# Linear-recurrence scan and top-capacity expert layer on one core: the early slot's weight fetches, first gathers and tile places rearranged

## Chip, cores and metric

One core of a Trainium2 chip (trn2). The metric is the device time of one execution in microseconds; the profile beside it is of one execution of the same program.

## What is computed

```python
# x, f_logit: (4, 5056, 256); lower_bound: (256,); w_gate: (256, 8); w1: (8, 256, 1024); w2: (8, 1024, 256)
f = lower_bound + (1 - lower_bound) * sigmoid(f_logit)
for t in range(S):                      # per batch
    h = f[:, t] * h + (1 - f[:, t]) * x[:, t]
    y[:, t] = h
x = y.reshape(20224, 256)
logits = x @ w_gate
# all (token, expert) pairs by falling logit: a token takes the expert if both are free,
# each expert holds cap = 20224 // 8 = 2528 tokens
for e in range(8):
    out[assigned == e] = relu(x[assigned == e] @ w1[e]) @ w2[e]
```

## The kernel before

The work has two stages.

**Scan stage.** The 158 tiles of 128 tokens are cut into 40 chunks of four tiles (the last has two). For each chunk SP loads `f_logit` and `x` (512 KB each) into a pool `pin` of four buffers for each of the two. In iteration `i` the program writes `load(i + 3)`, `fwd(i)`, `sig(i + 2)` and `back(i - 1)`. `sig` is a sigmoid on ScalarE and then a product `xl <- fl, xl` on GpSimd. `fwd` transposes both on TensorE (`pf`, `pb`) and runs the recurrence as a scan on VectorE (`g <- fg, pb`). `back` transposes the result back with the gate's weights beside it (`pr`), and VectorE and ScalarE copy it into a row tile `hr` with 256 values and 8 logits per token; GpSimd copies the logits of a chunk into the table `X` (the logit copies, `X <- hr`). `store` writes an `hr` tile to the buffer `hbuf` in DRAM (528 KB, SP's queue). A ring of 22 places of 4,224 bytes a partition holds the `hr` tiles; half a store is written per chunk (`SR = 0.5`), so 17 chunks are stored when the loads end and 23 follow at the end.

**The early slot.** From the first 72 tiles (`CE`) the program picks the expert that has the fewest tokens above a limit and takes 896 rows of it ahead of the full routing. `prep` finds the best expert of a token in pieces (reduction, comparison, product with `kc` (on GpSimd), reduction, comparison); `prep_step(n)` does up to `n` of these pieces at the end of an iteration. When `prep` of 72 columns is through, the generator `early` runs one step per iteration: counts, index of the expert's weights, the three weight fetches (`first_weights`, indirect transfers from GpSimd, 2 MB in all), ranks, and row numbers in four groups. At the end four indirect gathers from `hbuf` bring the first 512 rows (`XGE`); they wait for the stores of chunks 0 to 17.

**Second stage.** Nine slots (the early one, -1, and the experts in order of their routing) are worked in chunks of four or so tiles. For each chunk: transposes (`pt`, split into `xh` and `xl`), eight steps of a first product (`pw`, evacuated by ScalarE into `hh` and by VectorE into `hl`) and a second (`py`), then `y` tiles (two tiles of rows in one) that indirect stores from GpSimd write to `out`. Weights are split into a high and a low part by ScalarE and VectorE (`w1h`, `w1l`, `w2s`). The order of TensorE, VectorE and ScalarE is written out by the program; a small planner (`Pace`) books each engine's time by a formula and decides from it where evacuations and the routing's steps (the search for each expert's limit on VectorE) are put. The order of this stage's GpSimd issues follows a list.

**Places.** The second stage's tiles lie where the ring and the scan's work tiles lay, so a tile waits until what lay there has been stored or read. Counted from the ring's start in places of 4,224 bytes, the program before has these chunks on them at the end of the scan stage:

```
place  0  1  2  3  4  5  6  7  8  9 10 11 12 13 14 15 16 17 18 19 20 21
chunk 22 26 29 31 33 35 37 39 19 21 20 18 38 36 34 32 30 28 27 25 24 23
```

The second stage's pools follow each other from the ring's start in the order in which they are opened: `wa2` (one `w2s` of 16,384 bytes, the early slot's) on places 0 to 3, then 13 `y` tiles of 2,080 bytes, then `wb` (32,768 bytes), `hp` (5 `hh` and 5 `hl` of 2,048) and `xp` (two `xh`, two `xl` of 4,096), the last of these on the scan's work tiles.

Of the kernel before, what the change touches and what calls it, by code (L numbers as in the profile page):

```python
# [7 lines left out]
F32 = mybir.dt.float32  # L8
F32R = mybir.dt.float32r
# [97 lines left out]
def kernel(ctx: ExitStack, tc: tile.TileContext, x: bass.AP, f_logit: bass.AP,  # L107
# [3 lines left out]
    nc = Paced(tc.nc, pace)  # L111
    B, S, D = x.shape
# [4 lines left out]
    P = 128  # L117
    NT = N // P
    NC = 160
    NG = NC // E  # L120
    KT = 4
    ROW = D + E
    FB = F // P
# [19 lines left out]
    NCH = len(chunks)  # L143
    RING = 22
    SR = 0.5
# [15 lines left out]
    def rows_tile(dt):  # L161
        return pin.tile([P, KT * ROW], dt, name="fl")
# [411 lines left out]
    def ranks(c0, c1):  # L574
        em = EM[:, c0:c1]
        v.tensor_scalar(em, A1[:, c0:c1], ecode, 0.0, op0=OP.is_equal, op1=OP.add, accum_out=ecnt)
        v.tensor_tensor_scan(RSE[:, RW - c1 + c0:RW], onec[:, c0:c1], em, 0.0, op0=OP.mult, op1=OP.add)
# [15 lines left out]
    def early(wi, ids):  # L593

        def sums(ps):
            for g in range(CE // 8):
                nc.tensor.matmul(ps[:, :64], ones_b, O[:, 8 * g:8 * g + 8].rearrange("p c e -> p (c e)"), start=(g == 0),
                                 stop=(g == CE // 8 - 1))
        yield sums
        ps = beside[0]  # L600
        v.tensor_reduce(SC8, ps[:, :64].rearrange("p (c e) -> p e c", e=E), AX.X, OP.add)
        v.tensor_scalar(Q8, SC8, float(EARLY), 1.0e6, op0=OP.is_lt, op1=OP.mult)
        v.tensor_tensor(Q8, Q8, SC8, op=OP.add)
        v.tensor_reduce(few, Q8, AX.X, OP.min)
        yield
        v.scalar_tensor_tensor(Q8, Q8, few, kc, op0=OP.is_equal, op1=OP.mult)
        v.tensor_reduce(ecode, Q8, AX.X, OP.max)
        v.scalar_tensor_tensor(wi, wk, ecode, wb, op0=OP.mult, op1=OP.add)
        first_weights()
        yield  # L610
        ranks(0, CE)
        yield
        w = CE + 2

        def places(ps):
            nc.tensor.matmul(ps[:, w:w + 1], tri, ecnt, start=True, stop=True)
            nc.tensor.matmul(ps[:, :w], nsub, RSE[:, RW + 2 - w:], start=False, stop=True, skip_group_check=True)
        yield places
        ps = beside[0]
        st = ohp.tile([P, len(groups)], F32, name="st")  # L620
        for k in range(2):
            v.tensor_scalar(st[:, k:k + 1], ps[:, w:w + 1], -512.0 * k, None, op0=OP.add)
        v.tensor_copy(RAE[:, :w], ps[:, :w])
        v.tensor_tensor(RAE[:, w - 2:w - 1], ecnt, ps[:, w - 3:w - 2], op=OP.subtract)
        v.tensor_scalar(elim, ps[:, w:w + 1], -1.0, float(EARLY), op0=OP.mult, op1=OP.add)
        yield
        g1 = {}
        nb = EARLY // P
        for b0 in range(0, nb, 2):
            n = min(2, nb - b0)  # L630
            if b0 % 4 == 0:
                g1 = ohp.tile([P, 512], BF, name="g1")
                v.tensor_scalar(g1, IO, st[:, b0 // 4:b0 // 4 + 1], None, op0=OP.is_ge)
                yield

            def rows(ps):
                for b in range(n):
                    nc.tensor.matmul(ps[:, b * w:(b + 1) * w], g1[:, (b0 + b) % 4 * P:((b0 + b) % 4 + 1) * P],
                                     RAE[:, :w], start=(b == 0), stop=(b == n - 1), skip_group_check=True)
            yield rows  # L640
            for _ in blocks(beside[0], b0, n, w, 0, ids[:, b0:b0 + n], False):
                pass
            if b0 + n < nb:
                yield
# [55 lines left out]
    def sig(i):  # L700
        np_ = chunks[i][2]
        for a, b in halves(0, i):
            nc.scalar.activation(FT[i][:np_, a:b], FT[i][:np_, a:b], AF.Sigmoid, scale=-1.0)
        for a, b in halves(1, i):
            (nc.gpsimd if i else nc.vector).tensor_mul(XT[i][:np_, a:b], FT[i][:np_, a:b], XT[i][:np_, a:b])
# [49 lines left out]
            nc.gpsimd.tensor_copy(X[:, t0:t0 + n], HR[i][:, :n, P:P + E])  # L755

    ST = {}

    def store(i):
        t0, n, _ = chunks[i]  # L760
        ST[i] = nc.sync.dma_start(hbuf[t0 * P:(t0 + n) * P].rearrange("(n p) d -> p n d", p=P), HR[i][:, :n])

    def prep(c0, c1):
        e = min(c1, NT)
        x_, t_, m_, a_ = X[:, c0:e], TMP[:, c0:e], M0[:, c0:e], A1[:, c0:e]
        far = nc.gpsimd if c1 <= 128 else v
        v.tensor_reduce(m_, x_, AX.X, OP.max)
        yield 'k'
        v.tensor_tensor(t_, x_, bcl(m_, e - c0), op=OP.is_ge)
        yield 'k'  # L770
        far.tensor_tensor(t_, t_, bce(kc, e - c0), op=OP.mult)
        yield 'k'
        v.tensor_reduce(a_, t_, AX.X, OP.max)
        yield 'k'
        v.tensor_tensor(O[:, c0:e], bce(kc, e - c0), bcl(a_, e - c0), op=OP.is_equal)
        yield 'k'

# [1 line left out]

    def prep_step(n):  # L780
        while preps and n:
            if next(preps[0], None) is None:
                preps.pop(0)
            else:
                n -= 1

    sig(0)
    nc.vector.tensor_scalar(omlb, lbc, -1.0, 1.0, op0=OP.mult, op1=OP.add)
# [11 lines left out]
    w1v = w1.rearrange("e d f -> (e d) f")  # L800
    w2v = w2.rearrange("e (p j) d -> (e p) (j d)", j=FB)

    def first_weights():
        for n, (dst, src) in enumerate(((RAWE[0][:, 0], w1v), (RAWE[0][:, 1], w1v),
                                        (RAWE[1].rearrange("p j d -> p (j d)"), w2v))):
            nc.gpsimd.indirect_dma_start(out=dst, out_offset=None, in_=src,
                                         in_offset=bass.IndirectOffsetOnAxis(ap=WIE[:, n:n + 1], axis=0))

    WSE = []

    XGE = None
    for i in range(NCH + 1):
        job = next(est, None) if est is not None else None
        if i + LA - 1 < NCH:
            load(i + LA - 1)
            if i == 0:
                nc.gpsimd.memset(rest[-1], 0.0)
        if i < NCH:
            fwd(i)
        if i + 2 < NCH:  # L820
            sig(i + 2)
        if i >= 1:
            back(i - 1, job)
            while stored < min(i - 1, int(SR * (i - 1))):
                store(stored)
                stored += 1
        if i >= 4:
            build(2)
        if i >= NCH - 2:
            if i < NCH:  # L830
                WSE.append(pin.tile([P, FB, P], F32R, name="xl"))
            for h, j0 in (((0, 0),), ((1, 0),), ((0, 4), (1, 4)))[i - NCH + 2]:
                nc.scalar.activation(WSE[h][:, j0:j0 + 4], RAWE[0][:, h].rearrange("p (q j) -> p j q", j=FB)[:, j0:j0 + 4],
                                     AF.Identity, scale=omlb[:, h:h + 1])
        if i == NCH - 2:
            assert stored * KT >= CE
            XGE = rows_tile(F32R)
            for q in range(KT):
                nc.gpsimd.indirect_dma_start(out=XGE[:, q * ROW:(q + 1) * ROW].bitcast(F32), out_offset=None,
                                             in_=hbuf[:CE * P],  # L840
                                             in_offset=bass.IndirectOffsetOnAxis(ap=IDE[:, q:q + 1], axis=0),
                                             bounds_check=NT * P - 1, oob_is_err=False)
        upto = chunks[i - 1][0] // 8 * 8 if i else 0
        if done < CE and (upto - done >= 32 or upto >= CE):
            preps.append(prep(done, min(upto, CE)))
            done = min(upto, CE)
        elif CE <= done < CP and upto >= done + 32:
            preps.append(prep(done, done + 32))
            done += 32
        prep_step(99 if i == NCH else 3 if done == CE and upto < CE + 8 else PS if done < CE else 1 + (i > NCH - 3))  # L850
        if est is None and done >= CE and not preps:
            est = early(WIE, IDE)
# [21 lines left out]
    def route(r, rt, slot, free):  # L874
# [40 lines left out]
        else:  # L915
# [18 lines left out]
            v.scalar_tensor_tensor(MS, asg, cc, TR, op0=OP.is_equal, op1=OP.mult, accum_out=cM)  # L934
            spawn()
            yield 'DVE',
    for i in range(stored, NCH):
        store(i)
    pre.close()
    sched.close()  # L940
# [8 lines left out]
def moe(ctx, tc, g):  # L949
# [9 lines left out]

    def pool(name, bufs, **kw):  # L960
        return ctx.enter_context(tc.tile_pool(name=name, bufs=bufs, reuse_waits="tile", **kw))
    wa2 = pool("wa2", 1)
    YB = 13
    yp = pool("yp", YB)
    wb_ = pool("wb", 1)
    hp = pool("hp", 5)
    xp = pool("xp", 2)

    def y_tile():
        return yp.tile([P, 2 * D + 8], F32, name="y")[:, :2 * D].rearrange("p (r d) -> p r d", r=2)  # L970

    def x_tile():
        return rows_tile(F32R).rearrange("p (q r) -> p q r", q=4)
# [50 lines left out]
    def split(k):  # L1024
# [3 lines left out]
        for t, name in ((w1h, "w1h"), (w1l, "w1l")):  # L1028
            for h in range(len(t), 2):
                t.append(pin.tile([P, FB, P], F32R, name="xl") if k % 2 else  # L1030
                         wb_.tile([P, FB, P], F32R, name=f"{name}{h}"))
        w2s = (wa2 if k % 2 else wb_).tile([P, FB, 2, D], F32R, name="w2s")
        WS[k] = w1h, w1l, w2s
        pieces = []
        for j0, h in ((0, 0), (0, 1), (4, 0), (4, 1)):
# [382 lines left out]
```

## Time and profile before

| | us |
|---|---|
| median of 3 runs | 1196.99 (1195.78 to 1198.12) |
| the profiled execution | 1195.04 |
| its span | 1193.3 |
| TensorE busy | 1153.3 (97%) |
| VectorE busy | 791.0 (66%) |
| ScalarE busy | 540.8 (45%) |
| GpSimd busy | 459.2 (38%) |

How to read it: PE is TensorE's matmuls, PEld its weight loads, DVE VectorE, ACT ScalarE, POOL GpSimd, SP the queue that issues loads and stores. Busy shares are means over both stages, and a busy TensorE is not one at its peak. Nearly all instructions carry one line number (L100, a helper), so the names of the tiles tell them apart.

### The profile page before, as it was taken

To read this page: it belongs to the slowest core of one execution; us is meant where nothing else is said; L and a number is where in the kernel's file an instruction comes from. 1 tells how busy PE (TensorE), PEld (TensorE's weight loads), DVE (VectorE), ACT (ScalarE), POOL (GpSimd) and SP (SyncE) were. 2 spreads that over 40 slices of the span, in tenths; PEclk is the share of its full clock that TensorE was granted. 3 is DMA by queue.
4 is the path that set the end of the run, shared out by engine and by line. 5 is a ranking of instruction groups with operands and counts; after the bars stand their busy time and mean duration, and the time that the engine had idled before them with its cause. 6 is when DMAs were issued, how large, how long until landed. Compare 5 with 4: busy or idle time off the path is not lost. (4 is left out here: it accounts for less than half of the span.)

```text
span 1193.3 us, 22554 instructions
## 1 busy us (share of the span) xinstructions
PE 1153.3 (97%) x8829; PEld 1049.4 (88%) x8829; DVE 791.0 (66%) x1905; ACT 540.8 (45%) x1104; POOL 459.2 (38%) x463
## 2 busy tenths in 40 slices
PE   8999978999999999999999999999999999999997
PEld 7988967888888988998889888898889989999997
DVE  6998976677677867777977887867744542253221
ACT  7886853353426334532444444222544732252232
POOL 6766740423334334332433433333433333343322
PEclk9999989999999999999999999999999999999999
DMA  9998994121113113111311311111311311221110
GB/s 351 360 361 293 388 343 125 55 91 45 49 40 112 50 45 106 49 47 39 108 45 46 107 49 36 46 41 40 116 46 57 105 43 45 74 92 44 43 33 31
DMA packets 52447, 125.25 MB, mean 105 GB/s; under 512 B 8064, under 2 KB 28288, under 8 KB 51184
## 3 DMA queue, kind: packets, MB, share of 16 engines
q0 software_dynamic: 19248, 60.96, 15.9%
q1 hardware_dynamic: 32544, 62.78, 15.0%
q8 instruction: 71, 1.16, 0.4%
q14 instruction: 40, 0.33, 0.1%
q10 hardware_dynamic: 544, 0.01, 0.0%
HBM read 81.69 MB, written 42.10 MB: 104 GB/s over the span
## 5 line engine op out<-in xcount | busy, mean ns | idle before, releaser
L100 PE MATMUL py<-w2s,hh 128*128 128x256 f32 x2560 | 492.9, 288 | 0.5 <-ACT y L100 0.5
L100 ACT ACTIVATE hh<-pw 128x512 fp32r<-128x512 f32 (+3 forms) x328 | 190.7, 582 | 525.3 <-PE pw L100 450.8
L100 PEld LDWEIGHTS py<-w2s,hh 128*128 128x128 f32 x2560 | 408.0, 189 | 18.2 <-issue 1.2
L100 DVE SCALAR_TENSOR_TENSOR hl<-pw,hh 128x512 fp32r<-128x512 f32 (+3 forms) x328 | 219.6, 669 | 228.1 <-ACT hh L100 227.6
L100 PE MATMUL py<-w2s,hl 128*128 128x256 f32 (+1 forms) x1280 | 361.4, 282 | 0.0
L100 POOL DMA_INDIRECT out_dram<-y,ids x160 | 165.2, 1032 | 339.8 <-ACT hh L100 282.9
L100 POOL DMA_INDIRECT fl<-hbuf,ids x160 | 161.7, 1011 | 297.9 <-ACT hh L100 246.7
L100 PEld LDWEIGHTS py<-w2s,hl 128*128 128x128 f32 (+1 forms) x1280 | 241.4, 189 | 0.0
L100 PE MATMUL pw<-xh,xl 128*128 128x512 f32 (+3 forms) x672 | 232.2, 388 | 3.6 <-DVE hl L100 3.6
L100 PEld LDWEIGHTS pw<-xh,xl 128*128 128x128 f32 x672 | 125.7, 190 | 21.0 <-DVE hl L100 4.1
L100 PE MATMUL pw<-xl 128*128 128x512 f32 (+3 forms) x336 | 131.0, 390 | 0.0
L100 PE MATMUL pw<-xh,w1h 128*128 128x512 f32 (+1 forms) x320 | 126.5, 395 | 0.0
L100 PE MATMUL pw<-xl,w1h 128*128 128x512 f32 (+1 forms) x320 | 126.4, 395 | 0.0
L100 PE MATMUL pw<-xh,w1l 128*128 128x512 f32 (+1 forms) x320 | 125.5, 392 | 0.0
L100 POOL TENSOR_TENSOR xl<-fl,xl 128x1024 f32<-128x1024 f32 (+2 forms) x40 | 92.8, 2321 | 38.1 <-ACT fl L100 26.1
L100 DVE TENSOR_TENSOR_SCAN g<-fg,g,pb 128x512 f32<-128x512 f32 (+4 forms) x78 | 92.8, 1228 | 6.8 <-ACT fg L100 5.0
L100 PE MATMUL pr<-iw,g 128*128 128x136 f32 x632 | 82.6, 284 | 0.0
L100 PEld LDWEIGHTS pr<-iw,g 128*128 128x128 f32 x632 | 78.1, 193 | 0.2
L100 ACT ACTIVATE junk<-rt,r 128x158 bf16<-128x158 f32 (+1 forms) x153 | 59.3, 389 | 33.1 <-DVE r L100 30.3
L100 PEld LDWEIGHTS pw<-xh,w1l 128*128 128x128 f32 x320 | 60.2, 188 | 11.7
L100 PEld LDWEIGHTS pw<-xl 128*128 128x128 f32 x336 | 64.0, 190 | 6.0 <-DVE xl L100 0.3
L100 PEld LDWEIGHTS pw<-xh,w1h 128*128 128x128 f32 x320 | 60.7, 190 | 6.2
(216 smaller groups left out, 1396.7 us busy)
## 6 DMA issues: line engine op xcount, KB each, us to landing
hbuf<-hr SPq DMA_DIRECT2D x39, 528.0 KB, 9.7
fl<-in_f_logit_dram SPq DMA_DIRECT2D x38, 512.0 KB, 6.3
xl<-in_x_dram SPq DMA_DIRECT2D x38, 512.0 KB, 6.5
fl<-hbuf,ids POOLq DMA_INDIRECT x160, 2.8
out_dram<-y,ids POOLq DMA_INDIRECT x160, 2.4
fl<-in_f_logit_dram SPq DMA_DIRECT2D x3, 256.0 KB, 4.2
xl<-in_x_dram SPq DMA_DIRECT2D x3, 256.0 KB, 4.4
r<-in_moe_w_dram,wi POOLq DMA_INDIRECT x27, 5.4
```

The lines of the kernel that those rows point to most:

```text
L100: r = f(*args, **kw)
```

## The change

The weight fetches are issued in three steps of `early` instead of one. `prep` of the last eight early columns (64 to 72) ends an iteration's steps after each of its reductions, and its product with `kc` is on VectorE. The first four gathers are written one iteration earlier: the first ahead of GpSimd's last product, the others behind it and ahead of that iteration's logit copy. Stores follow a written order `TURN`, one more of them from iteration 31 on. The second stage's pools are opened in another order, with `xp` in two pools of one buffer, 12 `y` tiles of 2,144 bytes, and one `w2s` with 1,408 bytes of filling.

```diff
@@ early
-        first_weights()
+        first_weights(0)
         yield
         ranks(0, CE)
+        first_weights(1)
         yield
+        first_weights(2)
         w = CE + 2
@@
     ST = {}
+    TURN = [*range(18), 24, 18, 19, 20, 21, 23, 22, *range(25, NCH)]
@@ prep
-        far = nc.gpsimd if c1 <= 128 else v
+        few_ = c1 == CE
+        far = nc.gpsimd if c1 <= 128 and not few_ else v
         v.tensor_reduce(m_, x_, AX.X, OP.max)
-        yield 'k'
+        yield 'end' if few_ else 'k'
         v.tensor_tensor(t_, x_, bcl(m_, e - c0), op=OP.is_ge)
         yield 'k'
         far.tensor_tensor(t_, t_, bce(kc, e - c0), op=OP.mult)
         yield 'k'
         v.tensor_reduce(a_, t_, AX.X, OP.max)
-        yield 'k'
+        yield 'end' if few_ else 'k'
         v.tensor_tensor(O[:, c0:e], bce(kc, e - c0), bcl(a_, e - c0), op=OP.is_equal)
@@ prep_step
-            if next(preps[0], None) is None:
+            at = next(preps[0], None)
+            if at is None:
                 preps.pop(0)
             else:
-                n -= 1
+                n = n - 1 if at == 'k' else 0
@@
-    def first_weights():
-        for n, (dst, src) in enumerate(((RAWE[0][:, 0], w1v), (RAWE[0][:, 1], w1v),
-                                        (RAWE[1].rearrange("p j d -> p (j d)"), w2v))):
-            nc.gpsimd.indirect_dma_start(out=dst, out_offset=None, in_=src,
-                                         in_offset=bass.IndirectOffsetOnAxis(ap=WIE[:, n:n + 1], axis=0))
+    def first_weights(n):
+        dst, src = ((RAWE[0][:, 0], w1v), (RAWE[0][:, 1], w1v), (RAWE[1].rearrange("p j d -> p (j d)"), w2v))[n]
+        nc.gpsimd.indirect_dma_start(out=dst, out_offset=None, in_=src,
+                                     in_offset=bass.IndirectOffsetOnAxis(ap=WIE[:, n:n + 1], axis=0))
@@
+    def first_rows(q):
+        nc.gpsimd.indirect_dma_start(out=XGE[:, q * ROW:(q + 1) * ROW].bitcast(F32), out_offset=None, in_=hbuf[:CE * P],
+                                     in_offset=bass.IndirectOffsetOnAxis(ap=IDE[:, q:q + 1], axis=0),
+                                     bounds_check=NT * P - 1, oob_is_err=False)
@@ the scan stage's loop
         if i < NCH:
             fwd(i)
+        if i == NCH - 3:
+            assert stored * KT >= CE
+            XGE = rows_tile(F32R)
+            first_rows(0)
         if i + 2 < NCH:
             sig(i + 2)
+        if i == NCH - 3:
+            for q in range(1, KT):
+                first_rows(q)
         if i >= 1:
             back(i - 1, job)
-            while stored < min(i - 1, int(SR * (i - 1))):
-                store(stored)
+            while stored < min(i - 1, int(SR * (i - 1)) + (i > 30)):
+                store(TURN[stored])
                 stored += 1
@@
-        if i == NCH - 2:
-            assert stored * KT >= CE
-            XGE = rows_tile(F32R)
-            for q in range(KT):
-                nc.gpsimd.indirect_dma_start(out=XGE[:, q * ROW:(q + 1) * ROW].bitcast(F32), out_offset=None,
...
@@
-    for i in range(stored, NCH):
+    for i in TURN[stored:]:
         store(i)
@@ the second stage's pools
+    xp_ = [None, pool("xp1", 1)]
+    YB = 12
+    yp = pool("yp", YB)
     wa2 = pool("wa2", 1)
-    YB = 13
-    yp = pool("yp", YB)
     wb_ = pool("wb", 1)
     hp = pool("hp", 5)
-    xp = pool("xp", 2)
+    xp_[0] = pool("xp0", 1)
+
+    class Turns:
+        n = {}
+
+        def tile(self, shape, dt, name):
+            n = self.n[name] = self.n.get(name, -1) + 1
+            return xp_[n % 2].tile(shape, dt, name=name)
+    xp = Turns()
 
     def y_tile():
-        return yp.tile([P, 2 * D + 8], F32, name="y")[:, :2 * D].rearrange("p (r d) -> p r d", r=2)
+        return yp.tile([P, 536], F32, name="y")[:, :2 * D].rearrange("p (r d) -> p r d", r=2)
@@ split
-        w2s = (wa2 if k % 2 else wb_).tile([P, FB, 2, D], F32R, name="w2s")
+        if k % 2:
+            w2s = wa2.tile([P, FB, 2, D], F32R, name="w2s")
+        else:
+            w2s = wb_.tile([P, FB * 2 * D + 352], F32R, name="w2s")[:, :FB * 2 * D].rearrange("p (j m d) -> p j m d", m=2, d=D)
```

## Rows read from the trace of the kernel before

**Rows 1.** Windows by stage: start:end, length, busy by engine (count), PEclk, DMA share, GB/s

```profile
164.50:175.00 10.50, 2.08 (x9) 1.34 (x9) 3.84 (x7) 3.42 (x5) 5.57 (x7) 0.63 1.08 363
184.10:187.50 3.40, 3.33 (x10) 2.78 (x11) 2.86 (x9) 0.43 (x1) 0.00 (x0) 0.52 1.09 339
200.00:1190.00 990.00, 976.79 (x7404) 882.24 (x7403) 625.17 (x1606) 395.36 (x856) 343.56 (x337) 1.00 0.19 60
```

**Rows 2.** Timeline of ScalarE: start, length, operation, tiles (out<-in)

```profile
75.79 1.05 ACT L100 ACTIVATE fl<-fl 128x1024 f32<-128x1024 f32 x1
79.39 1.05 ACT L100 ACTIVATE fl<-fl 128x1024 f32<-128x1024 f32 x1
```

**Rows 3.** Timeline of VectorE, 75 to 107 us

```profile
75.90 2.44 DVE L100 TENSOR_TENSOR_SCAN g<-fg,g,pb 128x512 f32<-128x512 f32 x2
...
84.31 2.31 DVE L100 TENSOR_TENSOR TMP<-X,M 128x64 f32<-128x64 f32 x1
...
90.21 2.11 DVE L100 TENSOR_TENSOR O<-kc,A 128x64 bf16<-128x64 f32 x1
...
99.70 0.23 DVE L100 TENSOR_REDUCE SC<-pr 128x8 f32<-128x64 f32 x1 [1.68 <-ACT hr L100]
...
104.95 2.45 DVE L100 TENSOR_TENSOR_SCAN g<-fg,g,pb 128x512 f32<-128x512 f32 x2
```

**Rows 4.** Timeline of TensorE's matmuls; brackets: idle time before and its releaser

```profile
172.62 0.37 PE L100 MATMUL pt<-identr,fl 128*128 128x128 f32 x1 [1.41 <-DMA fl<-hbuf,ids]
...
184.17 0.73 PE L100 MATMUL pw<-xh,xl 128*128 128x512 f32 x1 [3.64 <-DVE hl L100]
```

**Rows 5.** Timeline of GpSimd in the dent

```profile
84.17 2.36 POOL L100 TENSOR_TENSOR xl<-fl,xl 128x1024 f32<-128x1024 f32 x1
...
89.88 2.36 POOL L100 TENSOR_TENSOR xl<-fl,xl 128x1024 f32<-128x1024 f32 x1
```

**Rows 6.** Timeline of VectorE around the start of the second stage

```profile
165.49 2.16 DVE L100 SCALAR_TENSOR_TENSOR xl<-r,omlb,xl 128x512 fp32r<-128x512 f32 x2
...
178.02 0.34 DVE L100 TENSOR_REDUCE M<-X 128x22 f32<-128x176 f32 x1
181.11 0.69 DVE L100 TENSOR_TENSOR w2s<-r,w2s 128x512 fp32r<-128x512 f32 x1 [2.75 <-ACT w2s L100]
...
183.43 0.68 DVE L100 SCALAR_TENSOR_TENSOR hl<-pw,hh 128x512 fp32r<-128x512 f32 x1
```

**Rows 7.** Timeline of GpSimd at the weight fetches (first of three, next product)

```profile
105.33 1.16 POOL L100 DMA_INDIRECT r<-in_moe_w_dram,wi  x1 [0.62 <-DVE wi L100]
...
109.05 2.37 POOL L100 TENSOR_TENSOR xl<-fl,xl 128x1024 f32<-128x1024 f32 x1
```

**Rows 8.** Timeline of GpSimd at the first gathers (first and last of four)

```profile
155.47 2.36 POOL L100 TENSOR_TENSOR xl<-fl,xl 64x1024 f32<-64x1024 f32 x1 [1.00 <-ACT fl L100]
...
161.19 0.21 POOL L100 COPY X<-hr 128x32 f32<-128x32 f32 x1 [2.75 <-DVE hr L100]
162.11 1.08 POOL L100 DMA_INDIRECT fl<-hbuf,ids  x1 [0.71 <-DMA hbuf<-hr]
...
166.21 1.23 POOL L100 DMA_INDIRECT fl<-hbuf,ids  x1 [0.30 <-issue]
```

**Rows 9.** Windows of the scan stage, columns as in rows 1

```profile
84.00:153.00 69.00, 64.22 (x551) 62.11 (x550) 63.72 (x107) 53.54 (x92) 46.67 (x39) 0.98 0.95 338
112.00:144.00 32.00, 31.33 (x277) 30.46 (x275) 30.48 (x54) 26.62 (x45) 23.75 (x19) 1.00 1.04 398
```

**Rows 10.** Timeline of ScalarE at the early slot's w2s

```profile
180.45 2.19 ACT L100 ACTIVATE w2s<-r 128x512 fp32r<-128x512 f32 x4 [4.67 <-DMA hbuf<-hr]
```

**Rows 11.** Timeline of SP's queue: the last 23 stores in one row

```profile
147.55 37.92 SPq L761 DMA_DIRECT2D hbuf<-hr  x23
```

**Rows 12.** Timeline of VectorE: one operation in two following search steps

```profile
236.25 0.23 DVE L100 TENSOR_TENSOR DM<-rt,bm 128x64 f32<-128x64 f32 x1 [0.85 <-PE rt L100]
...
243.19 0.23 DVE L100 TENSOR_TENSOR DM<-rt,bm 128x64 f32<-128x64 f32 x1 [1.35 <-PE rt L100]
```

More of the change, by code (lines that the diff above doesn't have):

```diff
@@ L834 @@
                                      AF.Identity, scale=omlb[:, h:h + 1])
-        if i == NCH - 2:
-            assert stored * KT >= CE
-            XGE = rows_tile(F32R)
-            for q in range(KT):
-                nc.gpsimd.indirect_dma_start(out=XGE[:, q * ROW:(q + 1) * ROW].bitcast(F32), out_offset=None,
-                                             in_=hbuf[:CE * P],
-                                             in_offset=bass.IndirectOffsetOnAxis(ap=IDE[:, q:q + 1], axis=0),
-                                             bounds_check=NT * P - 1, oob_is_err=False)
         upto = chunks[i - 1][0] // 8 * 8 if i else 0
```

## The prediction

> **What bounds the kernel now.** I read the windows view by stage first [rows 1]. From 200 us on TensorE is busy 976.8 of 990 us at full clock: that stage is a wall of matmuls, and the change does not touch their number. So whatever the change is worth must be earned before 200 us, and it arrives at the end only if it brings the first matmuls of the second stage forward. Ahead of the wall TensorE stands nearly still from 164.5 to 175 us (busy 2.08 of 10.5), and after a second stop, which ends at 184.1, the granted clock is 0.52 of full (the 1.2 GHz level) for 3.4 us.
>
> Next the timelines of single engines. In the scan stage a chunk takes 3.60 us when nothing disturbs it, as the spacing of two sigmoid passes shows [rows 2]; TensorE is full then, so 3.60 is its pace. But from the scan of chunk 18 (75.90) to that of chunk 24 (104.95) VectorE needs 29.05 us for six chunks [rows 3], where six paces are 21.6: a dent of 7.45 us. So there are three holes: the dent, the wait for the first rows (164.5 to 175), and the stop of 3.64 us that ends at 184.17 [rows 4].
>
> **Part 1, the dent.** VectorE works in order, and two tiny operations on 64 elements take 2.31 us (at 84.31) and 2.11 us (at 90.21) there [rows 3]. Both end with a GpSimd product: 84.17 + 2.36 = 86.53 and 89.88 + 2.36 = 92.24 [rows 5]. So a VectorE operation with two SBUF sources stood behind a GpSimd product, twice. Free of it such an operation should take 0.2 to 0.3 us; a reduction of 176 elements takes 0.34 [rows 6]. That makes 4.0 us for both.
>
> The Trainium skill (SBUF — State Buffer, Who interferes with whom) says the same and sharpens it: a VectorE instruction with two SBUF inputs and a GpSimd instruction that reads SBUF exclude each other for a whole instruction, and issue order decides who blocks. The rule speaks against this change, since the edit brings a third such operation (the product with kc) to VectorE; what that would make of the time stands under the first rival.
>
> The edit ends the step budget after each reduction of the last eight columns. In chunk 19's iteration only the reduction runs, so the scan of chunk 20 starts at about 84.35 instead of 86.54 (2.2 us). The comparison, the kc product and the second reduction then follow that scan and one copy, at about 87.1. GpSimd's next product can't start before its sigmoid: two paces after 79.39 [rows 2] is 86.6, and 1.05 for the pass and TensorE's own lag in the dent make it about 88.5 (an estimate). So the three fall in a gap of GpSimd of more than a microsecond. The last comparison falls one chunk on, around 91, just as that product ends. With both blocks gone (4.0 us), so goes the 1.68 us in which VectorE waits at 99.70 for a copy behind TensorE's late sums [rows 3]; the kc product on VectorE adds 0.25. Together 5.4 of the 7.45; the rest I leave.
>
> The weight fetches: three transfers in one go hold GpSimd from 105.33 until its product at 109.05 [rows 7]. One per chunk costs about 1.2 us each in gaps of about 1 us, such as the 1.00 us of idle time ahead of the product at 155.47 [rows 8]. I count nothing for it; if that cover is gone, 0.2 to 0.4 us a chunk for three chunks, and if the old burst did cost TensorE something, as much to gain.
>
> What the faster engine triggers: loads. Over 84 to 153 us, when the last load is in, the DMA engines moved 338 GB/s, so 23.3 MB; from 112 to 144 they went at 398 [rows 9]. The edit "+ (i > 30)" brings one store more (0.54 MB) ahead of the last load. 23.9 MB in 69 - 5.4 us is 376 GB/s, under the 398 seen, so the gain can be fed on average; but the 2 MB of weights now meet a queue that the dent has not emptied. I give back 1.0 (bounds 0, all loads fed, and 5.4, loads that stay at 338). Part 1: **-4.4 us**.
>
> **Part 2, the first gathers.** Before, GpSimd issues them behind the logit copies of chunks 36 and 37, the second of which waits 2.75 us for VectorE: from 162.11 to 167.44 [rows 8]. The last rows are there for the transpose at 172.62 [rows 4], 6.4 us after their issue began. Now the first gather goes into the idle microsecond ahead of the product at 155.47, which moves on by about 0.4 us; queued behind that product is TensorE's last transpose of x, a pace of work behind, so 0.4 us is covered (and costs 0.4 if not). The other three follow from about 158.5 at the same spacing of 1.37 us, so the last starts at 161.2 instead of 166.2 and lands at 167.6: **-5.0 us**. The copies come after them, near 162.5; nobody needs them before the reduction at 178.02 [rows 6]. The wait for the stores of chunks 0 to 17 is no new one: chunk 17 now leaves two iterations earlier. Right behind comes another limit: VectorE is busy with weight remainders until 165.49 + 2.16 = 167.65 [rows 6], so rows still earlier would bring no more than 0.1.
>
> **Part 3, the ring.** ScalarE's first w2s piece waits 4.67 us, to 180.45, for a store [rows 10]; VectorE needs w2s ahead of hl (183.43 [rows 6]) and TensorE needs hl's PSUM buffer (184.17 [rows 4]). The old w2s lies on ring places 0 to 3, so on chunk 31, the 15th of the last 23 stores; these leave in 37.92 us, 1.65 each [rows 11]. In the new layout xp1 (8,192 bytes) and twelve y tiles (25,728) come first, so w2s lies from place 8.03 to 11.91: chunks 19, 21, 20, 18. With chunk 24 put in, chunk 21's store is the 6th of those 23, nine earlier: 180.45 - 9 x 1.65 = 165.6, and ScalarE asks for it only at 180.45 - 4.67 = 175.8. The first hh tiles lie on places 20 and 21, chunks 24 and 23, which TURN sends early. So no store is waited for.
>
> What is late next is VectorE's written order: after the reduction (178.02 + 0.34) come the pieces that took from 181.11 to 183.43, 2.32 us, then hl, 0.7: the buffer is free at 181.4 instead of 184.17, measured from the same start. That is **-2.8 us**; 0.8 us of the stop stays. A stop that short should not drop the clock: the 3.4 us after it at 0.52 [rows 1] would take 1.8, **-1.6 us** (bounds 0 and 1.6).
>
> Twelve y tiles instead of thirteen, wider tiles and two xp pools of one buffer each: nothing. Two y pairs are made per chunk of the second stage, so twelve cover six chunks; if stores fell that far behind, ScalarE would wait at y with hh queued behind it.
>
> **Sum**: 4.4 + 5.0 + 2.8 + 1.6 = 13.8 us. The profiled execution took 1195.04 (span 1193.3 and 1.7 around it), so 1181.2; it stands 1.95 below the median of the three runs, and against that median the forecast is 1183.2. The likeliest case's own range is 1180 to 1187.
>
> **Rivals.**
> The block moves, or the loads starve (0.18): a two-source operation lands on a GpSimd product again, 2.1 to 2.3 us each time, or the loads stay near 338 GB/s. For it: three such operations now, margins of a few tenths. Against it: GpSimd's gap, the 398. Two blocks leave nothing of part 1's 4.4, one leaves 2.2; with about 1.0 left: 1186.6.
> The ring wait stays, so the change does not do what it says (0.05): if the places were filled in another order, w2s could lie on chunks 30 to 33. Chunk 33's store is two behind chunk 31's, 3.3 us later; parts 2 and 3 then turn from -9.4 into +3.3 and part 1 stays: 1195.9. Against: the old layout's wait fits chunk 31, so the order of the places is known.
> Slower (0.04): the second stage's order is written by a planner that books GpSimd's and VectorE's time. With these bookings moved it may put the search for the first slot later, and TensorE would stand for every search step that is missing when the early slot ends, 6.9 us each [rows 12]. It decides from two missing steps, which eat the gain; three make 1183.2 + 20.7 = 1203.9. Against: only some microseconds of bookings move, and TensorE's idle time after 200 us is 13 of 990 [rows 1].
>
> **How the numbers follow.** Forecast 0.73, the rivals as above. A difference under 0.2% (2.4 us) can't be told from none. Faster by more: forecast and first rival, 0.91; within 0.2%: the second, 0.05; slower: 0.04. The range takes in the first rival, the ends of the give-back and of the clock term, and some 2 us either way by which the planner's order may shift: 1178 to 1190.
>
> **What would show it.** Right: no 2 us operation on 64 elements between 84 and 92; the scan of chunk 24 near 99.6; GpSimd's first gather ahead of its last product; TensorE's first pw 9 to 10 us earlier; ScalarE's w2s directly behind xh, and a stop under 1 us. Wrong: VectorE operations of 2 us elsewhere, sigmoid passes that wait for loads after 100, a w2s that waits for a store, or new gaps of TensorE near 250.

## The result, and the profile after

The changed kernel takes 1185.65 us (median of 4 runs, 1185.2 to 1188.1) where the kernel before takes 1197.55 beside it (4 runs, 1195.78 to 1198.98): ratio 0.9906, 95% interval 0.9886 to 0.9925. That is 11.9 us less; the forecast was 13.8 less. The profiled execution took 1186.05 us with a span of 1184.2, 9.1 under the span before.

I follow the gain through the scan stage and the start of the second. Windows of the changed kernel first (start:end, length, busy by engine, granted clock, DMA share, GB/s), for [rows 1]:

```profile
172.50:175.90 3.40, 3.16 (x19) 2.86 (x20) 3.37 (x10) 1.14 (x2) 0.00 (x0) 1.00 1.10 340
190.00:1180.00 990.00, 975.85 (x7381) 879.71 (x7379) 622.69 (x1602) 395.40 (x855) 344.30 (x337) 1.00 0.19 60
```

The wall of matmuls is the same. The stretch behind the stop, which ran at 0.52 before, runs at 1.00.

**The dent.** Timeline of VectorE in the changed kernel, for [rows 3]:

```profile
83.84 2.44 DVE L100 TENSOR_TENSOR_SCAN g<-fg,g,pb 128x512 f32<-128x512 f32 x2
...
86.52 0.21 DVE L100 TENSOR_TENSOR TMP<-X,M 128x64 f32<-128x64 f32 x1
86.77 0.26 DVE L100 TENSOR_TENSOR TMP<-TMP,kc 128x64 f32<-128x64 f32 x1
87.06 0.22 DVE L100 TENSOR_REDUCE A<-TMP 128x8 f32<-128x64 f32 x1
87.19 2.44 DVE L100 TENSOR_TENSOR_SCAN g<-fg,g,pb 128x512 f32<-128x512 f32 x2
...
90.22 0.55 DVE L100 TENSOR_TENSOR O<-kc,A 128x64 bf16<-128x64 f32 x1
...
97.29 0.22 DVE L100 TENSOR_REDUCE SC<-pr 128x8 f32<-128x64 f32 x1
...
98.16 2.45 DVE L100 TENSOR_TENSOR_SCAN g<-fg,g,pb 128x512 f32<-128x512 f32 x2
```

And GpSimd's two products there, for [rows 5]:

```profile
83.81 2.37 POOL L100 TENSOR_TENSOR xl<-fl,xl 128x1024 f32<-128x1024 f32 x1
...
88.29 2.38 POOL L100 TENSOR_TENSOR xl<-fl,xl 128x1024 f32<-128x1024 f32 x1 [1.35 <-ACT fl L100]
```

The two operations that took 2.31 and 2.11 us take 0.21 and 0.55. The first three fall between the end of one product (86.18) and the start of the next (88.29); only the last comparison, 90.22 to 90.77, meets the tail of the second (to 90.67). From the scan of chunk 18 (75.53) to that of chunk 24 it is 22.63 us instead of 29.05.

**The loads.** ScalarE's sigmoids wait for their loads in four chunks between 98 us and the last one at 148.83, 5.0 us in all; before, one did, by 1.56 us. The timeline of ScalarE has chunks 31, 35 and 39:

```profile
119.46 1.06 ACT L100 ACTIVATE fl<-fl 128x1024 f32<-128x1024 f32 x1 [2.58 <-DMA fl<-in_f_logit_dram]
...
134.31 1.06 ACT L100 ACTIVATE fl<-fl 128x1024 f32<-128x1024 f32 x1 [1.60 <-DMA fl<-in_f_logit_dram]
...
148.83 1.05 ACT L100 ACTIVATE fl<-fl 64x1024 f32<-64x1024 f32 x1
```

**The first gathers.** GpSimd's timeline, for [rows 8]:

```profile
149.23 1.08 POOL L100 DMA_INDIRECT fl<-hbuf,ids  x1
150.62 1.01 POOL L100 DMA_INDIRECT fl<-hbuf,ids  x1 [0.30 <-issue]
151.93 1.00 POOL L100 DMA_INDIRECT fl<-hbuf,ids  x1 [0.30 <-issue]
152.96 2.37 POOL L100 TENSOR_TENSOR xl<-fl,xl 64x1024 f32<-64x1024 f32 x1
155.49 1.04 POOL L100 DMA_INDIRECT fl<-hbuf,ids  x1 [0.16 <-issue]
...
158.27 1.00 POOL L100 DMA_INDIRECT fl<-hbuf,ids  x1 [0.30 <-issue]
```

Here is something that the forecast did not have: three transfers stand ahead of the product, not one. The two at 150.62 and 151.93 belong to the second chunk's rows, which nobody needs yet: once an edge holds that chunk's gathers back, they are gone from there (experiment 6). The product and the other three first gathers go behind them. TensorE's timeline shows who pays, for [rows 4]:

```profile
155.39 0.46 PE L100 MATMUL pb<-ident,xl 64*128 64x64 f32 x4 [0.41 <-POOL xl L100]
...
161.74 0.28 PE L100 MATMUL pt<-identr,fl 128*128 128x128 f32 x1 [2.18 <-DMA fl<-hbuf,ids]
162.88 0.28 PE L100 MATMUL pt<-identr,fl 128*128 128x128 f32 x1 [0.86 <-DMA fl<-hbuf,ids]
164.09 0.37 PE L100 MATMUL pt<-identr,fl 128*128 128x128 f32 x1 [0.93 <-DMA fl<-hbuf,ids]
...
166.41 0.76 PE L100 MATMUL pw<-xh,xl 128*128 128x512 f32 x1
...
172.74 0.50 PE L100 MATMUL pw<-xh,xl 128*128 128x512 f32 x1 [0.34 <-DVE hl L100]
```

The first pw is 8.53 us earlier (174.94 before), and the stop of 3.64 us is 0.34.

**The ring.** ScalarE, for [rows 10]: w2s stands directly behind xh, though one hh behind it still waits for a store:

```profile
166.65 0.60 ACT L100 ACTIVATE xh<-pt 128x512 fp32r<-128x512 f32 x1 [1.56 <-PE pt L100]
167.15 2.18 ACT L100 ACTIVATE w2s<-r 128x512 fp32r<-128x512 f32 x4
...
171.12 0.60 ACT L100 ACTIVATE hh<-pw 128x512 fp32r<-128x512 f32 x1 [1.18 <-DMA hbuf<-hr]
```

Up to the fifth step's pw (188.64 before, 175.67 after) the profiled pair is 12.97 us apart. The end is only 9.1 apart, so 3.9 us are lost in the second stage of this pair; experiment 5 takes that up.

### The profile page after: what moved, and what is told of

Its sections match the earlier page's. It is cut to its first block, busy times and chain, and to the rows that moved or that the text cites. A ratio compares the mean times of both kernels' runs of the same rounds, so it can differ in the third digit from the quotient of the medians.

```text
span 1184.2 us, 22553 instructions
## 1 busy us (share of the span) xinstructions
PE 1151.3 (97%) x8829; PEld 1046.6 (88%) x8829; DVE 788.4 (67%) x1906; ACT 541.1 (46%) x1104; POOL 459.5 (39%) x462
## 4 chain that ended last, share of the span: by engine, by line
PE 89%; DMA 3%; issue 3%; DVE 2%; ACT 1%; POOL 1%; POOLq 0%; SPq 0%; DVEq 0%; ACTq 0%
PE py L100 38%; PE pw L100 36%; PE pr L100 5%; PE rt L100 4%; PE pb L100 3%; PE pf L100 2%; PE pt L100 2%; DVE g L100 1%; DMA fl<-in_f_logit_dram 1%; DMA hbuf<-hr 1%; DMA r<-in_moe_w_dram,wi 1%; DMA fl<-hbuf,ids 0%; POOL out_dram L100 0%; DMA xl<-in_x_dram 0%; ACT hh L100 0%
## 5 line engine op out<-in xcount | busy, mean ns | idle before, releaser
L100 PEld LDWEIGHTS pw<-xl,w1h 128*128 128x128 f32 x320 | 60.2, 188 | 6.2
```

What stands on the lines that cost most here:

```text
L100: r = f(*args, **kw)
```

## Experiments

For each run I split the way of the profiled execution to the second stage into four lengths: from the scan of chunk 18 to that of 24 (the dent), on to that of 39 (the loads), on to the first pw (the gathers), on to the first py (the ring). Ratios are to the kernel before on the same chip; its own median differs by chip (1193.5 to 1197.6), so runs are compared by ratio, or by time where they shared a chip: experiments 1 to 4 ran on one, 5 to 8 on a second, 9 to 11 on a third, 12 on a fourth. Each length is of one execution. From 24 to 39 the three rows with the old dent and the old count of stores have 57.04, 55.92 and 55.98 us, so a microsecond between rows is not yet an effect.

| kernel | ratio, 95% | 18 to 24 | 24 to 39 | to first pw | to first py |
|---|---|---|---|---|---|
| before | 1 | 29.05 | 57.04 | 12.95 | 11.88 |
| changed | 0.9906 (0.9886 to 0.9925) | 22.63 | 58.85 | 9.40 | 7.83 |
| changed, again | 0.9906 (0.9892 to 0.9920) | 22.63 | 58.32 | 9.69 | 7.93 |
| dent alone | 0.9956 (0.9943 to 0.9969) | 22.63 | 57.83 | 13.98 | 9.03 |
| gathers alone | 0.9995 (0.9984 to 1.0005) | 27.40 | 59.65 | 9.90 | 10.99 |
| ring alone | 0.9958 (0.9945 to 0.9971) | 27.39 | 55.92 | 12.66 | 7.95 |
| weight fetches alone | 0.9998 (0.9985 to 1.0010) | 27.39 | 55.98 | 13.76 | 9.83 |
| changed less gathers | 0.9914 (0.9900 to 0.9928) | 22.62 | 56.99 | 14.04 | 7.84 |
| changed less ring | 0.9952 (0.9935 to 0.9969) | 22.63 | 58.27 | 10.23 | 13.04 |
| kc on GpSimd | 0.9902 (0.9886 to 0.9918) | 22.62 | 59.07 | 10.17 | 7.84 |
| no early ends | 0.9939 (0.9925 to 0.9952) | 27.18 | 58.63 | 10.13 | 7.99 |
| ordering edge | 0.9893 (0.9877 to 0.9909) | 22.63 | 59.42 | 7.40 | 8.12 |
| ordering edge, again | 0.9909 (0.9894 to 0.9924) | 22.63 | 58.59 | 10.37 | 7.82 |
| edge, store late | 0.9904 (0.9888 to 0.9921) | 22.62 | 58.06 | 8.36 | 8.12 |

**1. The dent edit alone** (the kernel before with the diff's parts in prep and prep_step).

> The kernel before with part 1's edit of the reduction alone (step budget ended twice, last kc product on VectorE). My theory: the two blocked operations of 2.31 and 2.11 us go and with them the 1.68 us wait, so the scan of chunk 24 starts near 98.4 us instead of 104.95; loads give 1 to 2 us of it back, the scan of chunk 39 stands 4 to 5 us earlier, and since chunk 31's store moves up with the rest, the end does too: 4.4 us faster in the time (3 to 5.5). Rival, loads: the scan of chunk 24 is 6 us earlier but that of chunk 39 less than 2. Rival, ring: the first matmuls of the second stage come 5 us earlier, yet w2s still waits until about 180 us for its store, and the time gains less than 1.5 us.

0.9956, which is 5.3 us of 1197.4 (3.7 to 6.8; the two medians on that chip, 1193.2 and 1197.4, are 4.2 apart). The scan of chunk 24 comes 22.63 us behind that of 18, and w2s still waits 2.97 us, to 174.53. My theory held but for the wait of 1.68 us, which experiment 4 takes out; both rivals fell.

**2. The gathers alone** (first_rows and the store count `+ (i > 30)`).

> The kernel before with part 2 alone (first gathers earlier, one more store ahead of the last iterations). My theory: parts 2 and 3 are not additive. The first pw moves up by 3 to 4 us (not 5, because GpSimd's compiler-made order puts three gathers of the second chunk ahead of the last product and of the other first gathers), but ScalarE's w2s still waits for chunk 31's store, which the one store more brings forward by 1.65 us at most: 1 us faster in the time (0 to 2). Rival, additive: the stop moves with it, 3.5 us or more.

0.9995: 0.6 us, with none inside the interval. Timelines of GpSimd's last product and ScalarE's w2s:

```profile
160.12 2.37 POOL L100 TENSOR_TENSOR xl<-fl,xl 64x1024 f32<-64x1024 f32 x1
```

```profile
179.27 1.67 ACT L100 ACTIVATE w2s<-r 128x512 fp32r<-128x512 f32 x3 [4.93 <-DMA hbuf<-hr]
```

The first pw comes 1.4 us earlier (173.50), and then everything waits for the store. Here three more transfers got ahead of the product, which stands at 160.12 where it stood at 155.47 [rows 8]. That the parts do not add held, and the rival, 3.5 us or more, fell.

**3. The ring alone** (TURN, the pools, the widths).

> The kernel before with part 3 alone (places of the tiles and order of the stores). My theory: w2s goes directly behind xh, the first pw stays within 0.5 us of 174.94, the distance from the first pw to the fifth (13.70 us before: 174.94 to 188.64) falls by 4.4 us, 2.8 by the wait and 1.6 by the granted clock that no longer falls: 4.4 us faster in the time (3.5 to 5). Rival, the clock falls anyway in the shorter stop: 2.8. Rival, the ring wait stays or another store is waited for: 0 to 1.

0.9958: 5.0 us (3.5 to 6.6). ScalarE's w2s has no wait, and first pw to first py is 7.95 us where it was 11.88. The granted clock behind the steps (178.0 to 181.4) is 1.00. My theory held.

**4. The weight fetches alone.**

> The kernel before with the weight fetches one per chunk alone. My theory, as in the prediction: nothing, within 0.5 us either way. Rival, gain: the old burst held GpSimd from 105.33 to 109.05 and TensorE lost up to 1.2 us by it, which come back. Rival, cost: each fetch delays its chunk's product by 0.2 to 0.4 us, up to 1.2 us slower.

0.9998: nothing, as forecast. This run says more on the dent, which it leaves in. Its VectorE rows, for [rows 3]:

```profile
85.85 2.30 DVE L100 TENSOR_TENSOR TMP<-X,M 128x64 f32<-128x64 f32 x1
...
91.75 2.10 DVE L100 TENSOR_TENSOR O<-kc,A 128x64 bf16<-128x64 f32 x1
...
99.58 0.23 DVE L100 TENSOR_REDUCE SC<-pr 128x8 f32<-128x64 f32 x1
```

Both blocks are there, but the wait of 1.68 us ahead of SC is not. The profiled execution of the kernel before had a stretch at half the granted clock just there, and this one has none in the same place (windows of before, then of this run):

```profile
95.50:98.90 3.40, 3.40 (x24) 3.32 (x23) 2.52 (x3) 0.78 (x2) 2.52 (x2) 0.50 0.62 213
```

```profile
96.50:99.90 3.40, 3.40 (x38) 3.38 (x37) 3.34 (x7) 2.60 (x6) 2.41 (x2) 1.00 0.85 236
```

This run has such a stretch 5 us earlier (0.55 over 90.9 to 94.3), and the ring alone, with both blocks too, has none from 82 to 100 us; neither has the wait. So the wait went with that one stretch, not with the blocks. The old dent is 27.4 us long in three other executions, and the edit takes 4.8 of it.

**5. The changed kernel again.**

> The changed kernel unaltered, for a second profile and as the base for the next three on this chip. My theory on the 3.9 us that the first profile of it loses between 190 us and the end: 1.6 of them are a stretch at half the granted clock near 245 us, which may or may not be there in a second execution; if it is not, the difference from before is 13 us in the profiled pair. Rival: the stretch is there again, so it belongs to the kernel (the gap of 2.30 us ahead of it), and the difference stays near 10 to 12 us.

0.9906 once more. The pause of TensorE near 245 us is the same in both executions of the changed kernel (first profile, then this one):

```profile
244.09 0.31 PE L100 MATMUL rt<-RA,g 128*128 128x160 bf16 x2 [2.30 <-DVE RA L100]
```

```profile
245.40 0.31 PE L100 MATMUL rt<-RA,g 128*128 128x160 bf16 x2 [2.35 <-DVE RA L100]
```

But the clock falls behind the one and not behind the other (windows in the same order):

```profile
245.00:248.40 3.40, 3.40 (x16) 3.21 (x15) 2.98 (x7) 2.61 (x6) 0.00 (x0) 0.50 0.00 0
```

```profile
246.60:250.00 3.40, 3.40 (x26) 2.95 (x24) 3.18 (x10) 2.92 (x7) 0.00 (x0) 1.00 0.00 0
```

The py matmuls from the 192nd to the 480th take 85.7 us in the first and 84.0 here: 1.7 us for one such stretch (experiment 7 has it too, 85.6; 6 and 8 do not, 84.1 and 84.0). So the stretch belongs to an execution and not to the kernel, and the rival fell in that; the time is 11.2 us under the kernel before here.

From the first py to the end it is 1010.0 us in the first, 1004.8 here, and 1006.5 before. But this run was on another chip, where the kernel before itself takes 1193.5 us instead of 1197.55, so the 5.2 us between the two executions are not the stretch alone. On the 3.9 us two other comparisons bear. The profiled execution of the kernel before lies 2.5 us under its median and that of the changed kernel 0.4 above: the medians are 2.9 further apart than the two executions. And on one chip the length from the first py to the end is 1008.3 with the ring alone and 1009.4 to 1012.6 with the dent, the gathers or the fetches alone. So no loss by the change is shown there; how the 3.9 us divide is open.

**6. An ordering edge** that keeps the second chunk's gathers behind the first's.

```diff
-    issue(3)
+    for _ in range(3):
+        tc.add_manual_dep(issue().ins, g["last_rows"].ins.name,
+                          mybir.DependencyInfo(mybir.DependencyClass.NoSync, mybir.DependencyReason.DATA), reason="behind the first rows")
```

> The changed kernel with one ordering edge more: the gathers of the second chunk stand behind the four of the first on GpSimd. My theory, that part 2 fell short (3.55 instead of 5.0 us) because two of them were lifted ahead: the last product starts near 150.7 us instead of 152.96, the fourth first gather near 155.8 instead of 158.27, TensorE's first pw 1 to 2 us earlier than 166.41, and the time falls by 1.4 us (0.8 to 2). Rival: VectorE's weight remainders, which end at 164.2, set the start anyway, so the first pw moves by less than 0.5 and the time by less than 0.5.

1180.9 us (1179.96 to 1181.24) where the changed kernel on the same chip has 1182.3 (1181.43 to 1183.11): my theory held here, and experiment 11 repeats it. GpSimd's rows:

```profile
150.65 1.09 POOL L100 DMA_INDIRECT fl<-hbuf,ids  x1
151.78 2.38 POOL L100 TENSOR_TENSOR xl<-fl,xl 64x1024 f32<-64x1024 f32 x1
...
156.97 1.00 POOL L100 DMA_INDIRECT fl<-hbuf,ids  x1 [0.30 <-issue]
```

The product is directly behind the first gather, the fourth gather 1.3 us earlier than in the changed kernel, and the first pw 7.40 us behind the scan of chunk 39 instead of 9.40 or 9.69. TensorE then waits 1.62 us for VectorE's xl, which stands behind the weight remainders: that is the next limit.

**7 and 8. Which half of the dent edit works.** Experiment 7 puts the kc product back on GpSimd and keeps the early ends, 8 does the reverse.

```diff
-        far = nc.gpsimd if c1 <= 128 and not few_ else v
+        far = nc.gpsimd if c1 <= 128 else v
```

```diff
-        yield 'end' if few_ else 'k'
+        yield 'k'
```

> The changed kernel with the last kc product back on GpSimd (2.36 us or more there), the two ends of the step budget kept. My theory: the second reduction waits for that product on VectorE, in front of the next scan, so 2 to 3 us of the dent return: scan of chunk 24 near 100.5 to 101.5 instead of 98.16, time 1 to 2.5 us slower than the changed kernel, since loads had given part of it back already. Rival: the ends of the budget alone do it, GpSimd has room, less than 0.5 us slower.

> The changed kernel with the kc product on VectorE but the step budget as before (no early ends). My theory: the two comparisons fall on GpSimd's products again, or the kc product does: at least one operation of 2 us on 64 elements or more between 84 and 92 us, scan of chunk 24 at 101 to 103, time 1.5 to 4 us slower than the changed kernel. Rival: with the kc product off GpSimd the rest falls into other gaps and nothing is blocked, within 0.5 us.

On one chip: changed 1182.3, kc on GpSimd 1181.98, no early ends 1186.1 (1186.01 to 1186.68). In 7 my theory fell. GpSimd does that product in the gap that the early ends opened, and it takes 0.32 us, not the 2.36 of a big product that I had put in:

```profile
87.56 0.32 POOL L100 TENSOR_TENSOR TMP<-TMP,kc 128x64 f32<-128x64 f32 x1
```

In 8 it held, 3.8 us slower. Its VectorE and GpSimd rows:

```profile
83.49 2.30 DVE L100 TENSOR_TENSOR TMP<-X,M 128x64 f32<-128x64 f32 x1
...
88.07 0.40 DVE L100 COPY hr<-pr 128x264 f32<-128x264 f32 x1
...
88.89 2.37 DVE L100 TENSOR_TENSOR O<-kc,A 128x64 bf16<-128x64 f32 x1
```

```profile
83.35 2.35 POOL L100 TENSOR_TENSOR xl<-fl,xl 128x1024 f32<-128x1024 f32 x1
88.61 0.21 POOL L100 COPY X<-hr 128x32 f32<-128x32 f32 x1 [2.90 <-DVE TMP L100]
88.81 2.37 POOL L100 TENSOR_TENSOR xl<-fl,xl 128x1024 f32<-128x1024 f32 x1
```

Each blocked operation starts just behind a product and ends with it (85.79 and 85.70, 91.26 and 91.18). So the early ends are the edit, and with them in place it makes no difference to be seen where the kc product runs.

**9. The changed kernel less the gathers.**

> The changed kernel with the first gathers back behind the logit copies and without the one store more; dent edit, weight fetches and ring stay. By the sum of the single parts (0.44% for the dent, 0.42% for the ring, 0.05% for the gathers alone) the gathers would be worth about 0.6 us here too, so 1 us slower than the changed kernel at most: that is the rival. My theory: the gathers were worth nothing alone because w2s waited for its store in any case; with the ring in place the first rows are what TensorE stands for, so from the scan of chunk 39 to the first pw it takes 13 us again instead of 9.5, while the loads gain about 1 us by the store that is not ahead of them: 2.5 us slower than the changed kernel (1.5 to 4), ratio to the kernel before near 0.9927.

0.9914, 1187.49 us (1186.81 to 1188.57). The time fits the rival. The trace fits my theory: the first of the four transposes waits 4.16 us for its rows and the fourth comes at 167.29 (TensorE):

```profile
162.23 0.37 PE L100 MATMUL pt<-identr,fl 128*128 128x128 f32 x1 [4.16 <-DMA fl<-hbuf,ids]
...
167.29 0.37 PE L100 MATMUL pt<-identr,fl 128*128 128x128 f32 x1 [1.85 <-DMA fl<-hbuf,ids]
```

From the scan of chunk 24 to the first pw it is 71.0 us here and 68.3 and 68.0 in the two profiles of the changed kernel, so part 2 is worth 2.8 to 3.0 us at TensorE. At the end 1.0 is seen by the ratios, and the intervals allow a loss of 1.4 as well as a gain of 3.3; beside experiment 11, which has the gathers and the edge and ran on the same chip, it is 0.1 (1187.41). Open.

**10 and 11. The one store more behind the last load, and the edge again.** Both on one chip, beside 9; both have the edge of experiment 6, and 10 has this line besides.

```diff
-            while stored < min(i - 1, int(SR * (i - 1)) + (i > 30)):
+            while stored < min(i - 1, int(SR * (i - 1)) + (i > 35)):
```

> The changed kernel with the ordering edge (second chunk's gathers behind the first's) and the one store more taken from iteration 36 on instead of 31, so that it is issued behind the last load. My theory on part 1's give-back: those 0.54 MB stood ahead of the last loads, 1.2 to 1.4 us at 400 to 450 GB/s; from the scan of chunk 24 to that of 39 it takes 57.8 us (as with the dent edit alone) instead of 59.4, but the first gather now waits for a store that lands about 1 us later than it needs, so the gain at the first pw is 0.5 us (-0.5 to 1.2). Rival: the loads were late for the weights and the removed dent alone, the scans move by less than 0.5 us, and the first gather's wait costs 1 to 2 us.

> The changed kernel with the ordering edge, once more, as the base for the two runs beside it. Expected: ratio to the kernel before 0.989 again, 1.4 us under the changed kernel's 0.9906, and the first pw 7.4 us behind the scan of chunk 39. If the gain of 1.4 us was one chip's chance, the ratio stands at 0.9906.

Store late: 1185.85 us (1182.71 to 1188.08); the edge again: 1187.41 (1185.36 to 1187.98). ScalarE's sigmoids of chunks 35 and 39 with the store late:

```profile
132.51 1.06 ACT L100 ACTIVATE fl<-fl 128x1024 f32<-128x1024 f32 x1
...
147.59 1.05 ACT L100 ACTIVATE fl<-fl 64x1024 f32<-64x1024 f32 x1
```

No wait at 132.51. From the scan of chunk 24 (98.45) to the last sigmoid it is 49.1 us; without the gathers and their store it is 49.2, and in the changed kernel's two profiles 50.7 and 50.8. So that store costs the loads about 1.6 us (1.3 and 2.1 against the edge's own two profiles). The sigmoids of chunks 31 and 33 wait 2.09 and 0.54 us for their loads even so; what makes those late, the removed dent or the weight fetches, no run divides. At the first pw 0.4 us of it is left (66.4 from the scan of chunk 24, 66.8 with the edge alone in experiment 6): TensorE then waits 2.98 us for VectorE's xl, which is queued behind the weight remainders.

The edge's gain did not come back in the time of experiment 11: 0.9909, equal to the changed kernel within the interval. Its profile has a wait of ScalarE that no other trace here has, and that the profile puts to no engine:

```profile
160.79 0.39 ACT L100 ACTIVATE hr<-pr 128x264 f32<-128x264 f32 x1 [3.19 <-remote]
```

TensorE stood 2.00 us by it, and the first pw came 10.37 us behind the scan of chunk 39. What it was is open. GpSimd's order is that of experiment 6 (product at 151.03, fourth gather at 156.23), and the rows are there when TensorE asks for them. So the edge does what it says at GpSimd both times, beat the changed kernel by 1.4 us on one chip, and is not shown to be faster on another.

**12. The changed kernel less the ring.**

> The changed kernel with the old places of the tiles and the old order of the stores; dent edit, weight fetches and early gathers stay. My theory: without the ring the gathers are worth next to nothing, since w2s waits for its store either way. The first pw comes near 168 us, as in the changed kernel, but w2s is held until about 173 us and the first py comes 3 to 5 us later than in the changed kernel: ratio to the kernel before 0.9945 to 0.9955, that of the dent edit alone (0.9956). Rival, the parts add up: gathers and dent stay worth what they are in the changed kernel and only the ring's own 2.8 us of wait is missing, ratio 0.993 or less.

0.9952, the dent alone's 0.9956 within 0.04%. The first pw comes at 167.30, yet ScalarE's w2s and TensorE's next steps stand still (one row of each):

```profile
174.12 1.67 ACT L100 ACTIVATE w2s<-r 128x512 fp32r<-128x512 f32 x3 [5.98 <-DMA hbuf<-hr]
```

```profile
177.84 0.58 PE L100 MATMUL pw<-xh,xl 128*128 128x512 f32 x1 [4.28 <-DVE hl L100]
```

Rows that come earlier turn into a longer wait for the store. My theory held.

## Why the prediction was right, step by step

**Part 1, the dent: right, for the reason given, with one wrong entry.** The two blocks stood behind GpSimd's products and went when the operations were moved into the gap at 86.2 to 88.3 (experiments 1 and 8). The 1.68 us of the wait ahead of SC should not have been in the sum: it belonged to a half-clock stretch of that one execution (experiment 4). Counted with it, the profiled pair shows 6.4 where 5.4 was forecast; without it 4.8, where the forecast's other two entries make 3.75. No run divides that microsecond. That VectorE and GpSimd lock each other out, as the Trainium skill has it (SBUF — State Buffer, Who interferes with whom), the ends in experiment 8 bear out; that moving the third operation to VectorE would hurt, they do not, since it falls in the gap.

**The give-back: right in kind, mis-sized.** Forecast 1.0; from the scan of chunk 24 to that of 39 the two profiles of the changed kernel are 1.8 and 1.3 us longer than the profiled execution before, and up to 2.9 longer than the ring alone and the fetches alone, which have the old dent and the old count of stores. The store taken ahead of the last loads is about 1.6 of it (experiment 10); the rest is not divided. Dent and give-back together lie on both sides of the 4.4 forecast: where only the early ends differ, on one chip, the scan of chunk 39 comes 4.9 us sooner behind that of 18 and the time is 3.8 shorter (experiments 5 and 8); between the fetches alone and the dent alone, with one store less, it is 2.9.

**Part 2, the gathers: the mis-sized term.** Forecast 5.0; the two profiles show 3.6 and 3.3 from the scan of chunk 39 to the first pw. The step that failed is "the first gather goes into the idle microsecond ahead of the product at 155.47, which moves on by about 0.4 us", and with it "The other three follow from about 158.5": it took GpSimd's order to be the order in which the program writes the operations. In the profile it is not: two gathers of the second chunk, written later, stand ahead of the product and of the other first gathers. With them held back, the length is another 2.0 to 2.3 us shorter (experiment 6); in experiment 11 they are held back too, but a wait of ScalarE's covers it. And the sum took the parts as independent. Without the ring the gathers measure 0.05 and 0.04% (experiments 2 and 12), with none inside both intervals, since w2s waits for its store either way. The time shows about 1 us for them with it, too little for the intervals to tell from none.

**Part 3, the ring: right.** Forecast 2.8 and 1.6; 2.9 and 1.5 in the profiled pair (first pw to the fourth step's stop, and the fifth step behind it), 5.0 (3.5 to 6.6) in the time of the ring alone. Behind the stop, now 0.34 us, the clock is 1.00. "So no store is waited for" was not quite so: one hh waits 1.18 us for a store, to 171.12.

**The weight fetches and the twelve y tiles: nothing, right.** For the former experiment 4, for the latter the ring alone, whose time shows no cost of theirs.

**The sum: near, in part by luck.** Dent and ring alone multiply to 0.9956 x 0.9958 = 0.9914, which is just what the two measure together in experiment 9. The time shows 5.3, 5.0 and about 1 us, against 4.4, 4.4 and 5.0 forecast. The first two have the forecast inside their intervals and came out above it; the third fell short by some 4 us, and it is luck that the others made up part of that. None of the rivals came: no block moved, and TensorE is idle for 14 us of the 990 from 190 us on, where it was 13 [rows 1]. One of the forecast's own signs of being wrong did show, sigmoid passes that wait for loads after 100 us, but they did not eat the dent's gain (the 4.9 us above). The pause of TensorE near 250 is not new: before, it is 2.13 us long and ends at 256.99.

## What to carry to other kernels

Where an engine's order is left to a scheduler, read its compiled order before pricing a move: work that nobody needs yet can be put ahead of what was moved. When two waits end the same stage, an edit that shortens one may be worth nothing until the other is gone, so price the parts together. A tiny operation that starts behind another engine's big one and ends with it is a block; moving it into that engine's gap was enough here. And before a difference between two profiled executions is explained, see where each lies against the median of its kernel, and whether both ran on one chip.

## What the runs showed of the hardware

- Stretches of 3.4 us at half the granted clock fall at different places in executions of the same program: one behind TensorE's pause at 244 us in one, none behind the same pause in the other. One of them costs 1.7 us (experiments 5 to 8), as much as some of the effects studied here.
- A block costs both engines, the second one by way of the data (experiment 8). VectorE's row copy `hr` ends at 88.47, late because the scan ahead of it stood behind the blocked operation; GpSimd's logit copy, which reads `hr`, starts at 88.61 after 2.90 us of idle time, and the product behind it at 88.81, 1.06 us after its sigmoid ended. In the changed kernel that product starts 0.07 us after its sigmoid. The profile puts the 2.90 us down to `TMP`, which the copy doesn't read; but two other logit copies of this trace also start 0.13 us after `hr` ended.
- The same program differs by chip: the medians of the kernel before are 1193.5 and 1193.9 us on two chips (experiments 5 to 8 and 12) and 1197.3 and 1197.4 on two others (9 to 11 and 1 to 4), about as much as the dent edit is worth.
